# A hand-ordered attention and GELU feed-forward kernel: the order of its arithmetic from the tenth ff tile of batch 0 on is written anew

## The chip, the cores and the metric

One core of a Trainium2 chip. The time is device microseconds (us) of one execution of the whole program. PE is TensorE, DVE is VectorE, ACT is ScalarE, POOL is GpSimd, and SP is the engine that issues the transposing copies, the copies inside the chip and the stores; POOL issues the loads.

## The reference

Sparse attention for 4 batches of 8 heads, 768 positions and 64 columns a head, followed by a feed-forward layer on the 3072 rows of 512 columns:

```python
k_sum = k.reshape(B, H, nb, block, D).max(axis=3)      # blocks of 32 keys
v_sum = v.reshape(B, H, nb, block, D).mean(axis=3)
scores_l = scale * q @ k^T, kept where |i - j| < 16    # a narrow band
scores_s = scale * q @ k_sum^T + log(block)            # 24 block sums
a = softmax over both together
attn = a @ concat(v, v_sum)
...
x = attn.transpose(0, 2, 1, 3).reshape(B * S, H * D)   # 3072 x 512
h = x @ w_in                                           # 512 -> 2048
g = h * sigmoid(1.702 * h)
out = g @ w_out                                        # 2048 -> 512
```

## The kernel before

The kernel runs batch after batch, with the attention of one batch laid between the second product of the batch ahead of it. What is done, and in which order, stands in one long string, `ORDER` (line 35). It is a list of some thousand words. A program walks down it and issues for each word one small step. Every engine gets its steps in the order of the list and works strictly down its own share; engines wait for one another only through the data, through PSUM banks and through buffers that must come free. So moving a word changes the order only on the engines that this word uses, and a step that waits holds all that stands behind it on its engine.

A word is a name and its arguments, with dots between them. The names that matter here:

- `lk`, `lq`, `lv` (POOL): load the keys and queries of one head, or a part of the values, of one batch. `gate.b` (POOL) is a tiny copy that waits until a late transfer has landed, so that the loads behind it do not start earlier.
- `xk.s.g.e`, `xq.s.g` (SP): transposing copies that turn the keys and queries of batches 2 and 3 into the layout that the scores need. `d.half.g` (SP) does so for the attention's output. In batches 0 and 1 this is done on PE instead (`tk`, `tq`, `t`), with a copy out of PSUM (`kc`, `qc`, `c`).
- `xm`, `xa` (DVE): maxima of blocks of keys; `kr`, `kR` write them into the key layout, `kh`, `ka` copy the halo keys there. The last letter of these words is the engine (`d` DVE, `a` ACT, `g` POOL).
- `vm.b.bank` (PE): the block sums of the values, into a PSUM bank; `vb` (DVE): adds them up and writes them to SBUF; `sd`, `ha` (SP): copies of these sums and of the halo values into the value layout `vw`.
- `s.b.half.p.bank` (PE): scores of a pair of heads; `e` (ACT): exponential; `m` (DVE): mask; `v.b.half.p.bank` (PE): the product with the values; `nn.half.g` (DVE): division by the sums, for two pairs.
- `f.half.nt.k...bank` (PE): an ff tile, the first product of the feed-forward layer for 128 of the 2048 columns and half of a batch's positions (four matmuls of 384 columns; `k01` and `k23` are halves of it). `g.half.nt` (ACT): its GELU into `gT`.
- The second product uses Strassen's scheme with seven products in place of eight. `gs.j.n.what` (DVE, or POOL with a `g` at its end) makes the sums of `gT` that it needs, for `n` tiles from `j` on; `ws` the sums of the weights; `p.t.what` (PE) is one of the seven products (eight matmuls of 256 columns) and `x.t.what` takes it out of PSUM, together with what it has to be added to, into one of three output buffers `osb`; `o.b.t.half` (SP) stores such a buffer.
- `G` and `X` (ACT) load the tables for GELU and for the exponential ahead of use.

PSUM is used as four single banks, 0 to 3, and two pairs of banks, 4 and 5. A bank number of two digits means a pair: 42 and 52 are the whole pair 4 or 5, 40, 41, 50 and 51 one bank of it. A step that opens a bank waits until all that used it before has been read out.

A word's batch isn't always in it: the second product of batch 0 is issued among the attention of batch 1, and so on, so that `o.0.2.0` stores the last rows of the first half of batch 0 when the keys of batch 2 are about to be transposed.

Steps that appear later in this text, in the code: `vsum` (line 360) and `block_sums` (372) for `vm` and `vb`, `halos_all` (419) and `rows_all` (427) for `ka` and `kR`, `xk` (649), `xq` (655), `scores` (661), `values` (673), `normed2` (697), `ff` (721), `gelu` (737), `g_sums` (740), `product` (829), `taken` (852), `store` (869). The two lines that open a bank, and the two that rotate the output buffers:

```python
wide_now[where] = psum[where].tile([128, 1024 if dtype is F32 else 2048], dtype, name=name, tag="ps")
...
outp = ctx.enter_context(tc.tile_pool(name="outp", bufs=3))
now[t, o] = outp.tile([128, d_model], F32, name="osb", tag="osb")
```

The loop that walks the list:

```python
for word in ORDER.split():
    name, *args = word.split(".")
    ops[name](*[engines[a] if a in engines else a[1:] if a[0] == "k" else int(a) for a in args])
```

Of the kernel before, what the change touches and what calls it, by code (L numbers as in the profile page):

```python
# [49 lines left out]
f.1.0.k01.2 f.1.8.k23 ha.1.3.0 f.1.9.k0123.0 f.1.0.k23 ws.1.1 g.1.8 g.1.9 f.1.1.k0123.1 ws.2.0 f.1.2.k0123.3 g.1.0  # L50
f.1.3.k0123.2 g.1.1 ws.1.0 gs.0.2.0 ha.1.2.0 f.1.10.k0123.1 g.1.3 gs.0.2.1 f.1.4.k0123.2 g.1.2 gs.2.2.2 g.1.10 lv.1.5.0
gs.0.2.3 f.1.11.k0123.1 g.1.4 f.1.12.k0123.3 g.1.11 f.1.13.k0123.0 ws.3.1 tk.0.52 g.1.13 gs.2.2.0 g.1.12 kc.0.a
f.1.6.k0123.2 gs.0.2.2 gs.2.2.1 f.1.15.k0123.0 f.1.5.k0123.1 ws.3.0 g.1.6 g.1.5 tk.1.52 kc.1.a tk.2.42 kh.0.1.d ws.2.1
f.1.14.k0123.3 f.1.7.k0123.1 tk.3.52 gs.2.2.3 kc.2.a xm.0.1 tq.0.42 gs.4.2.0 g.1.15 kc.3.d p.0.2.0 g.1.7 g.1.14 gs.6.1.0
p.0.1.2 qc.0.a xm.1.1 tq.1.52 ha.1.1.0 gs.4.2.2 lq.2.0 x.0.1.a gs.4.2.1 gs.6.1.2 lq.2.2 gs.6.1.1 gs.7.1.0 ha.1.0.0
qc.1.a gs.6.1.3 lv.2.0.0 tq.2.42 p.1.1.3 qc.2.a gs.7.1.1 gs.4.2.3 p.0.5.1 x.0.5.a p.0.6 tq.3.52 kr.0.1.d s.1.0.0.42
x.0.6.a x.0.2.a gs.7.1.2 X gs.7.1.3 kr.1.1.d x.1.1.d xm.3.1 kh.2.1.g p.1.2.0 e.0.0 p.0.3 p.0.7 lq.2.3 m.0.0 x.0.3.a
x.0.7.a kh.1.1.d qc.3.d s.1.1.0.42 e.1.0 p.1.6 xm.2.1 vm.1.42 o.0.0.0.0.2 s.1.0.1.52 lv.2.5.0 e.0.1 kr.2.1.g kh.3.1.d
p.0.4 vb sd.1.1.0 x.0.4.a gate.1 s.1.1.1.52 e.1.1 lv.2.3.0 p.1.5.1 kr.3.1.d x.1.5.d x.1.2.a m.1.0 x.1.6.a s.1.0.2.52
# [20 lines left out]
lq.3.7 m.1.0 p.1.4 p.2.1.2 v.2.1.0.40 v.2.1.2.50 d.0.0 v.2.1.1.41 v.2.1.3.51 x.2.5.a x.2.1.d x.1.3.a lq.3.3 p.2.6  # L80
o.1.1.0.0.2 x.1.4.d d.0.1 p.2.3 nn.1.0 x.2.6.a p.2.7 nn.1.1 p.2.2.3 x.2.7.a x.2.2.a lv.3.4.0 d.1.0 lv.3.2.1 p.2.4
f.0.9.k01.3 x.2.3.a f.0.1.k01.0 G d.1.1 o.1.2.0.0.2 f.0.1.k23 f.0.8.k01.1 f.0.8.k23 f.0.9.k23 x.2.4.a f.0.0.k01.2
f.0.0.k23 lk.3.6 g.0.1 g.0.9 g.0.8 f.1.1.k0123.0 f.1.8.k0123.1 g.0.0 f.1.9.k0123.3 g.1.1 g.1.9 g.1.8 f.1.0.k0123.2
f.0.10.k0123.0 g.0.10 gate.2 g.1.0 gs.0.2.2 xk.1.1.0 f.1.2.k0123.1 gs.0.2.0.d gs.0.2.1 xk.1.0.1 f.1.10.k0123.3 g.1.2
# [20 lines left out]
g.1.15 gs.7.1.0 gs.7.1.1.g p.0.5.1 x.0.1.d p.0.2.0 p.0.6 x.0.6.a x.0.2.a gs.6.1.3 gs.4.2.2.d x.0.5.d gs.7.1.2 p.1.1.3
p.0.7 p.2.2.0 x.0.7.a x.1.1.a gs.0.2.3.d gs.7.1.3.g gs.4.2.3 p.0.4 x.0.4.a p.0.3 x.0.3.a p.1.2.2 x.1.2.a p.1.6
o.3.0.0.0.2 x.1.6.a p.1.5.1 x.1.5.d o.3.0.1.0.2 p.2.1.2 x.2.1.d p.1.3 x.2.2.a p.1.7 x.1.3.a p.2.6 x.2.6.d x.1.7.a
o.3.1.0.0.2 p.2.5.1 p.2.7 x.2.5.a p.2.3 x.2.7.a p.1.4 p.2.4 x.2.3.a x.1.4.d x.2.4.d o.3.2.1.1.2 o.3.2.0.0.2 P7.0
o.3.1.1.0.2 o.3.2.1.0.1
# [854 lines left out]
```

## Time and profile before

| | |
|---|---|
| median of 3 runs | 212.04 us (211.33 to 214.41) |
| the profiled execution | 211.7 us |
| its span, first to last instruction | 210.0 us |
| mean granted TensorE clock | 0.996 |
| PE busy | 200.4 us |
| DVE busy | 130.8 us |
| ACT busy | 114.3 us |
| POOL busy | 109.1 us |
| ff tiles (`ph`), 512 matmuls | 86.1 us |

All instructions of a compute engine go through one helper, so that the profile gives line 28 for nearly all of them; they are told apart by the tiles that they write and read. `ph` is an ff tile's PSUM bank, `poA`, `poB` and `poC` are those of the second product, `ps_s` of the scores, `ps_av` of the product with the values, `ps_vs` of `vm`. A row of the order of time reads: start, length, engine, operation, what is written and read, how many in a row, and in brackets how long the engine had been idle and what ended that.

### The profile page before, as it was taken

How to read it: one execution, taken by the hardware profiler on the slowest of the kernel's cores; microseconds unless marked ns; L12 is line 12 of the kernel's file. 1: busy time of each engine (PE TensorE's matmuls, PEld its weight loads, DVE VectorE, ACT ScalarE, POOL GpSimd, SP SyncE). 2: the span in 40 equal slices, each digit the busy share in tenths (PEclk: the TensorE clock that was granted, in tenths of full speed). 3: DMA queues.
4: the chain of work that ended last, by engine and by line, in shares of the span. 5: the costliest groups of instructions: out<-in, count | busy, mean ns of one | idle time of the engine just before them, and what ended most of it. 6: DMA issues, size and time to landing. Idle time of an engine off the chain costs nothing.

```text
span 210.0 us, 5880 instructions
## 1 busy us (share of the span) xinstructions
PE 200.4 (95%) x2440; PEld 145.8 (69%) x2440; DVE 130.8 (62%) x311; ACT 114.3 (54%) x227; POOL 109.1 (52%) x157
## 2 busy tenths in 40 slices
PE   7998798999999999999999999999999999999993
PEld 5656554667887886556788865657888865668882
DVE  5577873798997871168997822694888500166342
ACT  2473885659666736676764336567670157671100
POOL 7999972399982998448949422431000000863000
PEclk9999999999999999999999999999999999999998
DMA  4999999999999999999999999939215920000214
GB/s 67 162 166 189 209 213 221 182 144 122 99 134 199 156 177 183 130 126 141 148 166 204 142 227 180 187 29 169 50 53 139 160 105 0 0 3 0 100 53 150
DMA packets 96458, 27.74 MB, mean 132 GB/s; under 512 B 85024, under 2 KB 93488, under 8 KB 96432
## 3 DMA queue, kind: packets, MB, share of 16 engines
q0 software_dynamic: 70800, 13.64, 82.7%
q1 hardware_dynamic: 25632, 13.74, 33.2%
q8 instruction: 19, 0.31, 0.6%
q14 instruction: 7, 0.06, 0.1%
HBM read 27.26 MB, written 6.29 MB: 160 GB/s over the span
## 4 chain that ended last, share of the span: by engine, by line
PE 79%; POOL 12%; DMA 5%; issue 1%; DVE 1%; SPq 0%; POOLq 0%; DVEq 0%
PE ph L28 36%; PE poA L28 19%; PE poB L28 10%; PE poC L28 5%; PE ps_s L28 3%; PE ps_av L28 3%; DMA vw<-vw 2%; POOL mk L28 2%; DMA out_dram<-osb 2%; POOL v0n L28 2%; POOL w_in_sb L28 2%; POOL kb L28 2%; POOL kx L28 2%; POOL qb L28 1%; PE ps_t L28 1%
## 5 line engine op out<-in xcount | busy, mean ns | idle before, releaser
L28 PE MATMUL ph<-xT,w_in_sb 128*128 128x384 f16 x512 | 86.1, 326 | 0.4 <-DVE osb L28 0.4
L28 ACT ACTIVATE gT<-ph 128x384 f16<-128x384 f32 x128 | 56.1, 495 | 30.6 <-PE ph L28 29.9
L28 PEld LDWEIGHTS <-w_in_sb 128*128 128x128 f16 x512 | 49.2, 98 | 32.4 <-issue 0.9
L28 PEld LDWEIGHTS <-gs 128*128 128x128 f16 x384 | 36.5, 98 | 4.6
L28 DVE TENSOR_TENSOR gs<-gT 128x768 f16<-128x768 f16 (+1 forms) x36 | 17.5, 498 | 29.1 <-ACT gT L28 29.0
L28 POOL TENSOR_TENSOR gs<-gs,gT 128x768 f16<-128x768 f16 (+1 forms) x6 | 8.8, 1461 | 41.8 <-PE ph L28 32.7
L28 POOL DMA_DIRECT2D kb<-in_k_dram x28 | 23.1, 842 | 13.7 <-DMA w_out_sb<-in_moe_w_out_dram 6.4
L28 ACT ACTIVATE a_sb<-ps_s 128x768 bf16<-128x768 f32 x32 | 24.8, 808 | 9.5 <-PE ps_s L28 9.3
L28 PEld LDWEIGHTS <-gT 128*128 128x128 f16 x288 | 27.3, 98 | 3.6
L28 POOL DMA_DIRECT2D vw<-in_v_dram x36 | 25.7, 752 | 5.0 <-DMA w_out_sb<-in_moe_w_out_dram 1.7
L28 PE MATMUL poA<-ws,gs 128*128 128x256 f16 x192 | 24.8, 273 | 0.0
L28 POOL DMA_DIRECT2D qb<-in_q_dram x28 | 23.8, 867 | 1.8 <-issue 0.9
L28 DVE TENSOR_TENSOR a_sb<-a_sb,mk 128x768 bf16<-128x768 bf16 x28 | 14.7, 550 | 3.0 <-ACT a_sb L28 2.2
L28 DVE TENSOR_TENSOR x<-ps_av,rc 128x768 f16<-128x768 f32 (+1 forms) x18 | 15.6, 869 | 0.6
L28 ACT ACTIVATE s<-poA 128x256 f32<-128x256 f32 x14 | 5.4, 382 | 19.3 <-PE poA L28 18.6
L28 PE MATMUL poB<-ws,gs 128*128 128x256 f16 x96 | 12.5, 273 | 0.0
L28 PE MATMUL poC<-w_out_sb,gT 128*128 128x256 f16 x96 | 12.5, 273 | 0.0
L28 PE MATMUL poA<-w_out_sb,gT 128*128 128x256 f16 x96 | 12.4, 273 | 0.0
L28 PE MATMUL poB<-w_out_sb,gs 128*128 128x256 f16 x96 | 12.4, 273 | 0.0
L28 PE MATMUL poA<-ws,gT 128*128 128x256 f16 x96 | 12.3, 273 | 0.0
L28 DVE TENSOR_REDUCE ka<-kx 128x48 bf16<-128x1536 bf16 x4 | 7.0, 1750 | 7.4 <-DMA kx<-kb 7.4
L28 ACT ACT_TABLE_LOAD x8 | 10.3, 1283 | 0.9 <-PEq L948 0.8
(102 smaller groups left out, 219.0 us busy)
## 6 DMA issues: line engine op xcount, KB each, us to landing
out_dram<-osb SPq DMA_DIRECT2D x23, 256.0 KB, 2.9
kb<-in_k_dram POOLq DMA_DIRECT2D x24, 96.0 KB, 6.0
qb<-in_q_dram POOLq DMA_DIRECT2D x24, 96.0 KB, 5.0
vw<-in_v_dram POOLq DMA_DIRECT2D x36, 64.0 KB, 5.1
w_out_sb<-in_moe_w_out_dram POOLq DMA_DIRECT2D x4, 512.0 KB, 14.8
w_in_sb<-in_moe_w_in_dram POOLq DMA_DIRECT2D x3, 512.0 KB, 11.3
vw<-vs SPq DMA_DIRECT2D x6, 198.0 KB, 3.9
kb<-in_k_dram POOLq DMA_DIRECT2D x4, 192.0 KB, 4.4
```

The costliest lines, as they stand in the source:

```text
L28: r = f(*a, **kw)
```

## The change

Only the string `ORDER` changes. It holds the same 1002 words before and after, none added, none taken away, none with another argument: every step keeps its engine, its bank and its size. Up to the word `lq.1.4` (the 180th) nothing moves at all, and on PE the first ten ff tiles and `f.0.11` keep their places. Behind that the order of the steps on PE, ACT and DVE is new. The order of all copies that SP issues and of all loads that POOL issues is the same as before. On POOL some steps of arithmetic (`kh.2.1`, `kr.2.1`, `ka.0`, and a few of the `gs`) stand elsewhere between the loads.

Much of it are exchanges of neighbours. The wider moves, as the words run on one engine:

```diff
 # PE, batch 0, first values
-f.0.8 f.0.9 f.0.11 f.0.10 v.0.1.0 v.0.1.1 v.0.1.2 f.0.13 f.0.12 t.1.0 v.0.1.3 f.0.15 f.0.14 t.1.1
+f.0.8 f.0.9 f.0.11 v.0.1.0 v.0.1.2 v.0.1.3 v.0.1.1 f.0.15 f.0.10 f.0.13 f.0.12 t.1.0 t.1.1 f.0.14
 # PE, end of batch 0's second product
-v.1.0.2 v.1.0.3 v.1.1.2 v.1.1.3 p.2.4 f.0.1.k01 t.0.1 f.0.9.k01 f.0.8.k01 f.0.0.k01
+p.2.4 v.1.0.2 v.1.0.3 p.2.2 t.1.0 f.0.0.k01 t.0.1 f.0.9.k01 f.0.1.k01 v.1.1.2 v.1.1.3 f.0.1.k23 p.2.3
 # DVE, the same place
-nn.0.0 nn.1.0 x.2.7 x.2.2 m.1.2 x.2.3 nn.0.1 nn.1.1 c.0.1 c.1.1
+nn.0.0 m.1.3 x.2.7 nn.1.0 nn.0.1 x.2.2 c.0.1 nn.1.1 x.2.3 c.1.1
 # DVE, ahead of batch 2's scores
-xa.0.0 gs.2.2.0 vb gs.2.2.1 gs.2.2.3 xa.1.0 gs.7.1.0 kR.0
+xa.0.0 vb gs.2.2.0 gs.2.2.1 gs.2.2.3 gs.4.2.2 gs.0.2.3 gs.4.2.0 gs.7.1.0 xa.1.0 kR.0
 # PE, batch 1's second product
-p.1.2 p.1.7 p.1.3 p.1.4 p.2.1 v.2.1.0 v.2.1.2 v.2.1.1 v.2.1.3 p.2.6
+p.1.2 p.1.3 p.1.6 v.2.1.2 v.2.1.0 v.2.1.1 v.2.1.3 p.2.1 p.1.7 p.2.6
 # PE, batch 2's ff tiles
-f.1.3 vm.3 f.0.13 f.0.3 ... f.1.15 f.0.7 s.3.0.1 s.3.0.0 p.0.2 p.0.1 p.1.2 p.0.5
+f.1.3 f.0.11 f.0.4 ... f.0.14 f.1.6 vm.3 f.1.15 f.0.15 f.1.7 p.0.1 p.1.2 s.3.0.1 s.3.0.0 p.0.5
 # DVE, the same place
-gs.0.2.3 xa.0.1 vb xa.1.1 kR.1 gs.2.2.0 ka.1 gs.2.2.3 gs.6.1.0 gs.6.1.1 gs.4.2.0
+gs.0.2.3 gs.6.1.0 ka.1 gs.6.1.2 kR.1 gs.6.1.1 gs.4.2.0 vb x.0.1 gs.7.1.0
 # POOL
-lq.2.0 lq.2.2 lv.2.0.0 kh.2.1 lq.2.3 lv.2.5.0 kr.2.1 gate.1
+lq.2.0 lq.2.2 kh.2.1 lv.2.0.0 kr.2.1 lq.2.3 lv.2.5.0 gate.1
 # PE, last batch
-f.1.7 f.1.15 f.0.15 p.0.1 p.0.5 p.0.2 p.0.6
+f.1.7 f.1.15 f.0.14 p.0.5 p.0.1 p.1.1 p.0.6 f.0.15 p.0.7 p.0.2
```

`P7.0`, which only gives memory back, stands somewhat earlier in the list, and `late`, which opens two pools, ahead of `m.1.3` as before.

More of the change, by code (lines that the diff above doesn't have):

```diff
@@ L50 @@
[L50 to L59, printed above, removed]
@@ L80 @@
[L80 to L84, printed above, removed]
@@ L105 @@
[L105 to L109, printed above, removed]
+lk.1.5 lk.1.6 lq.1.2 lk.1.7 m.1.1 lq.1.1 lv.1.0.0 lq.1.4 cv.1 lq.1.5 lq.1.7 lv.1.3.1 f.0.8.k0123.2 lq.1.6 lv.1.0.1
@@ new lines @@
+lv.1.2.0 lv.1.1.0 lv.1.1.1 lv.1.4.0 lv.1.2.1 lv.1.4.1 late g.0.8 f.0.9.k0123.3 f.0.11.k0123.0 g.0.11 m.1.3 v.0.1.0.40
+v.0.1.2.50 v.0.1.3.51 v.0.1.1.41 f.0.15.k0123.0 ws.0.0 g.0.9 f.0.10.k0123.1 nn.1.0 f.0.13.k0123.3 nn.1.1 g.0.10
+f.0.12.k0123.2 g.0.13 t.1.0.42 t.1.1.52 f.0.14.k0123.1 ha.1.3.0 g.0.12 c.1.0.d g.0.14 f.1.0.k01.2 f.1.8.k01.3 c.1.1.d
+f.1.8.k23 ws.1.0 g.1.8 ha.1.2.0 f.1.1.k0123.1 g.0.15 ws.0.1 g.1.1 f.1.0.k23 f.1.2.k0123.3 f.1.10.k0123.1 g.1.0 lv.1.3.0
+ws.3.0 g.1.2 f.1.3.k0123.2 g.1.10 f.1.9.k0123.0 ws.1.1 g.1.3 ws.3.1 f.1.11.k0123.1 f.1.4.k0123.2 g.1.9 f.1.13.k0123.0
@@ new lines @@
+x.0.6.a gs.4.2.3 x.0.5.a lq.2.0 qc.1.a xm.1.1 p.0.3 s.1.0.0.42 xm.3.1 tq.3.52 kr.1.1.d e.0.0 kh.3.1.d p.0.7 vm.1.42
+qc.3.d s.1.0.1.52 x.0.3.a ha.1.0.0 lq.2.2 o.0.0.0.0.2 x.0.7.a p.1.2.0 vb kh.2.1.g kr.3.1.d x.1.2.a p.0.4 p.1.5.1 x.1.6.a
+e.0.1 lv.2.0.0 m.0.0 s.1.1.1.52 x.0.4.a e.1.1 xm.2.1 m.1.0 x.1.5.d kr.2.1.g sd.1.1.0 s.1.0.3.42 e.0.3 p.1.7 s.1.0.2.52
+p.2.1.2 lq.2.3 e.0.2 lv.2.5.0 p.1.3 x.1.7.a x.2.1.a gate.1 lv.2.3.0 s.1.1.3.42 lv.2.1.1 m.0.1 s.1.1.2.52 m.0.3 lk.2.0
+e.1.2 lk.2.2 m.0.2 lv.2.2.0 e.1.3 p.2.6 sd.1.0.0 p.1.4 x.1.3.a v.1.0.0.50 m.1.2 o.0.0.1.0.2 lv.2.2.1 x.2.6.a lk.2.3
@@ new lines @@
+x.2.2.a f.0.0.k01.2 lv.3.2.1 x.2.3.a f.0.9.k01.3 f.0.8.k01.1 d.1.1 f.0.8.k23 g.0.8 f.0.9.k23 f.0.1.k23 g.0.9 o.1.2.0.0.2
+lk.3.6 f.0.0.k23 g.0.0 f.1.8.k0123.1 xk.1.1.0 xk.1.0.1 g.0.1 g.1.8 f.1.9.k0123.3 f.1.0.k0123.2 gate.2 g.1.9 g.1.0
+f.1.1.k0123.0 o.1.1.1.0.2 g.1.1 gs.0.2.0.d f.1.10.k0123.3 f.0.2.k0123.2 g.1.10 g.0.2 f.0.10.k0123.0 f.1.2.k0123.1
+xk.1.1.1 g.0.10 f.1.11.k0123.3 f.0.13.k0123.0 f.0.3.k0123.2 g.1.2 f.1.3.k0123.1 g.0.13 g.0.3 xk.1.0.0 g.1.3
+f.0.11.k0123.0 xa.0.1 g.1.11 f.0.4.k0123.2 gs.0.2.1 lq.3.6 gs.0.2.2 f.1.12.k0123.3 g.0.11 f.0.12.k0123.1 xa.1.1 lv.3.5.1
@@ L110 @@
+p.2.1.2 x.1.5.d p.1.3 x.2.1.d o.3.0.0.0.2 o.3.0.1.0.2 p.2.2.0 p.1.7 p.2.6 x.1.3.a x.1.7.a x.2.6.d o.3.1.0.0.2 p.2.5.1
+x.2.5.a p.2.7 p.2.3 x.2.2.a x.2.7.a o.3.2.1.1.2 p.1.4 x.2.3.a o.3.2.0.0.2 x.1.4.d p.2.4 o.3.1.1.0.2 x.2.4.d o.3.2.1.0.1
 """
```

89 lines of the change are left out of this document (45 added, 44 removed).

## The prediction

> **What bounds the kernel now.** I read the page first, then busy time by stretch, then the chain that ended last, then the order of time on PE and DVE.
>
> ```profile
> PE 200.4 (95%) x2440; PEld 145.8 (69%) x2440; DVE 130.8 (62%) x311; ACT 114.3 (54%) x227; POOL 109.1 (52%) x157
> ```
>
> In the second view the first number after the stretch is its length and the next is PE's busy time in it.
>
> ```profile
> 33.40:34.80 1.40, 0.35 (x9) 0.25 (x10) 0.22 (x1) 0.73 (x2) 0.60 (x1) 1.00 1.24 217
> 34.80:100.30 65.50, 65.50 (x803) 46.48 (x800) 46.72 (x99) 41.91 (x83) 48.62 (x66) 1.00 1.78 150
> 100.30:122.50 22.20, 21.77 (x353) 18.66 (x353) 18.34 (x43) 10.72 (x18) 13.85 (x19) 1.00 1.92 177
> 122.50:123.20 0.70, 0.29 (x3) 0.11 (x2) 0.57 (x2) 0.38 (x1) 0.00 (x0) 1.00 1.28 284
> 123.20:206.40 83.20, 83.20 (x832) 60.92 (x831) 42.34 (x91) 40.26 (x85) 17.76 (x15) 1.00 0.44 87
> 206.40:210.00 3.60, 0.00 (x1) 0.00 (x0) 0.42 (x1) 0.00 (x0) 0.00 (x0) 0.79 0.38 139
> ```
>
> From 33.4 us on, where the changed part begins, PE is idle 1.05 + 0.43 + 0.41 = 1.89 us before its last matmul, at a granted clock of 1.00, and then 3.6 us pass for the last eviction and store. The change keeps every matmul. So at most 1.9 us can be won, under 1%, while any new wait of PE is paid in full. The question is which of the three gaps close and where new ones open.
>
> **The prices.** The chain of waits gives PE's, in the order start, length, what; behind it two rows of PE's timeline.
>
> ```profile
> 39.33 7.51 PE ph L28 x44
> ...
> 75.52 0.88 PE ps_av L28 x48
> ...
> 131.71 0.53 PE ps_vs L28 x48
> ...
> 167.26 20.80 PE ph L28 x128
> 188.06 0.87 PE poA L28 x8
> ```
>
> ```profile
> 33.73 0.19 PE L28 MATMUL ps_av<-vw,a_sb 128*64 128x65 bf16 x1 [0.28 <-DVE ws L28]
> 34.69 0.73 PE L28 MATMUL ps_av<-vw,a_sb 128*64 128x65 bf16 x35 [0.77 <-DMA vw<-vw]
> ```
>
> An ff tile (4 matmuls) is 20.80/128 x 4 = 0.65 us, a `p` 0.87, a `v` 0.88/4 = 0.22, the value sums `vm` 0.53. With these I add up the PE list of both orders.
>
> **First place, `v.0.1.x`.** The second matmul of `v.0.1.0` waits for a halo copy that releases it at 34.69. Nothing ahead of that copy changes. Before, four ff tiles (8, 9, 11, 10) run first and PE waits 0.28 + 0.77; after, tile 10 stands behind the `v`, so PE arrives 0.65 earlier and waits 0.65 more. Some returns: from 34.69 to 39.33 PE runs 47 `v` matmuls, four ff tiles and two `t` in seven pieces in 4.64 us, against 0.86 + 2.60 + 0.67 = 4.13 at the dense price (a `t` at 0.33, an estimate: six matmuls of 128 columns by the 20.80/128 of 384 columns). Half as many changes of kind should give back some 0.2 of these 0.5. Term: +0.45 (0.3 to 0.65).
>
> **Second place, the transposes for batch 2.** In the SP list nothing moves, but what it waits for does. `xk.0.0.0`, the first of six transposing copies, stands behind `o.0.2.0` and `o.0.2.1`. DVE's rows, then SP's:
>
> ```profile
> 75.56 0.43 DVE L28 TENSOR_TENSOR osb<-poB,s 128x256 f32<-128x256 f32 x1 [0.32 <-PE poB L28]
> ...
> 77.24 0.22 DVE L28 RECIPROCAL rc<-ps_av 128x12 f32<-128x12 f32 x1
> 77.50 0.96 DVE L28 TENSOR_TENSOR x<-ps_av,rc 128x768 f16<-128x768 f32 x1
> ```
>
> ```profile
> 77.82 0.33 SPq L28 DMA_DIRECT2D out_dram<-osb  x1
> 78.41 8.40 SPq L28 DMA_TRANSPOSE kx<-kb  x4
> 86.90 10.33 SPq L28 DMA_TRANSPOSE qT<-qb  x2
> ```
>
> Before, `x.2.3` is done at 75.99, `x.2.4` lets `o.0.2.1` go at 77.82, and `xk` starts at 78.41. After, `x.2.3` stands on DVE behind `nn.1.1`, which needs `v.1.1.3`, which ended at 76.40. Ahead of that `v` PE now also runs `p.2.4`, three half ff tiles and `t.0.1`, and no longer `p.2.3`: +0.87 + 0.98 + 0.33 - 0.87 = 1.31. With the 0.45 it ends at 78.2; `nn.1.1` takes 77.50 + 0.96 - 77.24 = 1.22, `x.2.3` 0.43, so `o.0.2.0` goes at 79.85, `o.0.2.1` 0.59 later, `xk` another 0.59 later: 81.0, 2.6 later than before. Queued behind it on SP are all six transposes and the six `ha`/`sd` copies of batch 2. The last two transposes, alone in their windows, and the last `ha`:
>
> ```profile
> L28 SPq DMA_TRANSPOSE qT<-qb x1: 5776/5776/5776, 86.9 to 86.9; - x1
> ...
> DMA to landing us min/median/max: 12.1/12.1/12.1
> ```
>
> ```profile
> L28 SPq DMA_TRANSPOSE qT<-qb x1: 1518/1518/1518, 95.7 to 95.7; - x1
> ...
> DMA to landing us min/median/max: 7.6/7.6/7.6
> ```
>
> ```profile
> L28 SPq DMA_DIRECT2D vw<-vw x1: 1337/1337/1337, 102.2 to 102.2; - x1
> ...
> DMA to landing us min/median/max: 8.6/8.6/8.6
> ```
>
> `xq.0.1` lands at 103.3. Its first reader before was `s.2.0.2`:
>
> ```profile
> 100.79 0.66 PE L28 MATMUL ps_s<-qT,kx 64*128 64x64 bf16 x24 [0.43 <-issue]
> ...
> 104.11 0.52 PE L28 MATMUL ps_s<-qT,kx 64*128 64x64 bf16 x24
> ```
>
> It has 0.8 us to spare. After, `s.2.0.3` takes this place at the same depth of the PE list, due at 104.35 (0.45 from above, 0.2 less from the next term). How much of the 2.6 reaches the landing no row shows. At 0 it lands at 103.3 and costs nothing; in full at 105.9 and costs 1.55, and the last `ha`, landing at 102.2 + 8.6 = 110.8 before, comes as late for `v.2.0.2`, due near 112.0 then. SP was free for `xq.0.1` at 86.90 + 5.78 = 92.7 and issued it at 95.7, so a shift of 2.6 still fits ahead of that issue, which speaks for less than the full shift. I take half: 104.6, so 0.25, and 0.35 for the `ha`. Term: +0.6 (0 to 2.7).
>
> On this the Trainium skill, "DMA: Bandwidth & Descriptors", section "Queues, rings and completion order", says that each DMA engine takes turns, packet by packet, between the queues that have work. By that rule loads drain faster while SP is silent and the late transposes share with fewer of them; the term would be nearer 0.3 than 0.6. No row of this execution separates the two.
>
> **Third place, `s.2.0.x`.** The 0.43 at 100.79 is `kR.0` on DVE, late behind `xa.1.0`. After, `p.0.1` stands ahead of the scores too. From the end of `vm.2` to the first score PE has eight ff tiles and two `p`, 6.95 us; DVE has `vb`, six sums of 768 columns, one of 384, `xa.1.0` and `kR.0`, by the rows of the fourth place 1.52 + 2.8 + 0.27 + 1.75 + 0.45 = 6.8. A near tie, at worst 0.4 more when the late transposes hold `xa.0.0` ahead of `vb`. Term: -0.2 (-0.43 to +0.3).
>
> **The gap at 122.5.**
>
> ```profile
> 122.63 0.42 DVE L28 TENSOR_TENSOR osb<-poC,s 128x256 f32<-128x256 f32 x1 [1.16 <-DMA out_dram<-osb]
> ```
>
> `x.2.2` waits for a free output buffer, that is for `o.1.1.0`, issued after `x.1.3`. `p.1.3` moves 1.75 up the PE list (two `p`), so the buffer comes free about as much earlier, and the wait was 1.16. Term: -0.4 (-0.4 to 0).
>
> **Fourth place, `vm.3` and `vb` of batch 3.** Before, `vm.3` runs at 131.6 and `vb` right after it. After, `vm.3` is ten us further down the PE list, behind `f.1.6`, and on DVE `vb` stands behind `gs.6.1.0` (which needs `f.1.6`), `ka.1`, `gs.6.1.2`, `kR.1`, `gs.6.1.1` and `gs.4.2.0`. `vm.3` fills PSUM bank pair 5, which `s.3.0.0.52` takes next, so that score must wait for the end of `vb`. DVE's rows; a later row's start shows how fast each is followed:
>
> ```profile
> 135.44 0.28 DVE L28 COPY vpart<-ps_vs 128x128 f32<-128x128 f32 x1
> ...
> 136.96 1.75 DVE L28 TENSOR_REDUCE ka<-kx 128x48 bf16<-128x1536 bf16 x1
> 138.75 0.53 DVE L28 COPY kx<-ka 128x576 bf16<-128x576 bf16 x2
> 139.20 0.55 DVE L28 TENSOR_TENSOR gs<-gT 128x768 f16<-128x768 f16 x1
> 139.66 2.10 DVE L28 COPY kx<-kx 128x320 bf16<-128x320 bf16 x3
> 141.69 0.55 DVE L28 TENSOR_TENSOR gs<-gT,gs 128x768 f16<-128x768 f16 x1
> ...
> 143.78 0.35 DVE L28 TENSOR_TENSOR gs<-gT,gs 128x384 f16<-128x384 f16 x1
> 144.05 0.35 DVE L28 TENSOR_TENSOR gs<-gT 128x384 f16<-128x384 f16 x1
> 144.61 0.36 DVE L28 TENSOR_TENSOR gs<-gT 128x384 f16<-128x384 f16 x1 [0.21 <-ACT gT L28]
> ```
>
> ```profile
> 144.09 1.26 ACT L28 ACTIVATE gT<-ph 128x384 f16<-128x384 f32 x3 [0.69 <-PE ph L28]
> ```
>
> One gelu is 0.495 and is handed on in 0.03 (144.09 to 144.61). So from the end of `f.1.6`: gelu with both handovers 0.57; sum of 384 columns 0.27; `ka.1` 141.69 - 139.66 = 2.03; sum 0.27; `kR.1` 0.45; sum 0.27; sum of 768 columns 0.46; `vb` 136.96 - 135.44 = 1.52; handover 0.05: 5.89 us. PE meanwhile: `vm.3` 0.53, three ff tiles 1.95, `p.0.1` and `p.1.2` 1.74, one `s`, half of the 0.52 at 104.11, 0.26: 4.48. PE waits 1.4 us. Queued behind it: `p.0.5` and all that follows. Nothing hides it, since PE has no spare time later. Upper end with each sum at its full length and `ka` at 2.10: 2.0; lower end with 0.1 for each of three changes of kind on PE: 1.1. The scores' `sd` copies come ten us later as well but stay ahead of `v.3.0.2`, eight `p` further on. Term: +1.4 (1.1 to 2.0).
>
> **What costs nothing.** On POOL the loads keep their order; `kr.2.1` now stands ahead of two of them (some 1.5 us), and behind them `gate.1` holds the queue anyway:
>
> ```profile
> 67.04 0.18 POOL L28 COPY gate<-vw 32x1 bf16<-32x1 bf16 x1 [4.16 <-DMA vw<-vs]
> ```
>
> In the last batch `p.0.5` follows `f.0.14` directly; its eighth matmul comes 0.65 + 0.76 = 1.41 after `f.1.15`, the gelu and two sums that it needs take 0.57 + 0.27 + 0.36 + 0.05 = 1.25. No wait, 0.16 to spare; 0.4 if that cover is gone.
>
> **Sum.** 0.45 + 0.6 - 0.2 - 0.4 + 1.4 = +1.85 us. The profiled execution took 211.7 us, a span of 210.0 and 1.7 around it: 213.55. The median of the runs shown, 212.04, is 0.34 above that execution, so I predict 213.9.
>
> **Rivals.** *Late transposes decide.* If `xq.0.1` meets the traffic that `xq.0.0` met and takes 12.1 us instead of 7.6, it lands at 95.7 + 12.1 = 107.8, and `s.2.0.3` waits 3.45 instead of the 0.6: +4.7, 216.7. For it: both lengths are in the trace, and the loads of batch 3 begin just there. Against it: before, the same copy had 7.6 at the same issue time. It makes the whole slower by over 2% (4.24 us) when the landing passes 107.35, or 106.75 with the fourth place at its upper end. *The waits fall away.* If `vb` costs PE nothing, because bank pair 5 or the DVE list is free earlier than I add up, and the transposes land as before: 0.45 - 0.2 - 0.4, 211.9. For it: only 1.4 us of cover is missing. Against it: DVE runs strictly down its list, and `ka.1` cannot pass `gs.6.1.0`. *Faster by over 2%* would need 4.24 us where PE has 1.89 of idle time to give; only a shift of the measurement could show it. That the change does not do what it says, and every wait stays as it was, gives 212.0 and is counted with the second rival.
>
> **Chances.** Forecast (213 to 216) 0.44, late transposes 0.36, waits fall away 0.18, faster by over 2% 0.02. Two per cent is about what a measurement of this kernel can tell from no change. So: faster 0.02, within 2% 0.62, slower 0.36. The range runs from the second rival, 212.0, to the first with a little of the full shift on top, 217.6.
>
> **What would show it.** Right: PE idle before the `v` at 33 us near 1.7; `xk` starting near 81; no gap before the ff tiles near 123; PE waiting some 1.4 us for DVE `vs` between the two scores at 146 to 148. Wrong: no gap there, or PE idle over 2 us at `s.2.0.3` near 105, which is the first rival; or a gap in a place not named here, which means a dependence that I did not see.

## The result and the profile after

The changed kernel takes 213.51 us (median of 22 runs, 211.82 to 215.57), the kernel before 212.18 (22 runs, 210.23 to 214.74) on the same chip. Both have some executions in a slower state (3 of these 22 for the changed kernel); without them the ratio is 1.0085, 95% interval 1.0061 to 1.0108, which is 1.8 us, while the two medians differ by 1.3. So the change makes the kernel slower, by less than 2%. The profiled execution took 213.88 with a span of 212.2, 2.2 more than the span before. The forecast was +1.85 and 213.9. So the total was met, but only two of its six terms were: some were too large by about as much as others were too small, and that is luck.

Section 1 of the page after, TensorE's and the other engines' busy time:

```profile
PE 200.3 (94%) x2440; PEld 145.2 (68%) x2440; DVE 133.8 (63%) x311; ACT 116.5 (55%) x227; POOL 110.7 (52%) x157
```

PE does the same work (200.4 before). DVE has the same 311 instructions and needs 3.0 us more for them (130.8 before), POOL 1.6 more for its 157. An unchanged count with more busy time means that single operations became longer. Busy time by stretch of the changed kernel (after the stretch its length, then PE's busy time):

```profile
32.50:36.00 3.50, 2.32 (x56) 1.74 (x57) 1.80 (x3) 0.68 (x2) 0.82 (x1) 1.00 1.24 210
36.00:100.30 64.30, 64.20 (x760) 45.94 (x758) 45.26 (x100) 42.97 (x84) 48.37 (x66) 1.00 1.74 150
100.30:123.50 23.20, 21.30 (x348) 17.87 (x347) 19.15 (x42) 10.98 (x19) 14.05 (x19) 1.00 1.94 169
...
145.00:160.00 15.00, 14.89 (x250) 12.33 (x249) 14.21 (x37) 10.42 (x16) 1.16 (x1) 1.00 0.28 68
160.00:208.60 48.60, 47.56 (x409) 35.67 (x407) 23.49 (x41) 17.81 (x41) 10.85 (x7) 1.00 0.24 64
```

The waits behind these losses, in PE's timeline of the changed kernel (in brackets the idle time ahead of a row and what ended it):

```profile
32.94 0.19 PE L28 MATMUL ps_av<-vw,a_sb 128*64 128x65 bf16 x1 [0.67 <-DMA vw<-vw]
33.87 0.92 PE L28 MATMUL ps_av<-vw,a_sb 128*64 128x65 bf16 x47 [0.73 <-DMA vw<-vw]
...
102.62 0.67 PE L28 MATMUL ps_s<-qT,kx 64*128 64x64 bf16 x24 [1.90 <-issue]
...
192.49 0.61 PE L28 MATMUL poA<-ws,gs 128*128 128x256 f16 x4 [0.90 <-DVE gs L28]
```

Against the execution before: first place 1.40 instead of 1.05; batch 2's first score 1.90 instead of 0.43; the gap of 0.41 near 123 gone; between 145 and 160 us, where 1.4 was forecast, 0.11; and 0.90 at `p.0.6` of the last batch, a place that the prediction doesn't name. +0.35 + 1.47 - 0.41 + 0.11 + 0.90 = +2.4, against 2.2 in the span.

What DVE does ahead of the first score of batch 2 (its timeline, the changed kernel):

```profile
95.39 0.56 DVE L28 TENSOR_TENSOR gs<-gT 128x768 f16<-128x768 f16 x1
95.98 0.69 DVE L28 TENSOR_TENSOR gs<-gs,gT 128x768 f16<-128x768 f16 x1
96.71 0.69 DVE L28 TENSOR_TENSOR gs<-gT,gs 128x768 f16<-128x768 f16 x1
97.32 1.57 DVE L28 TENSOR_TENSOR gs<-gT 128x768 f16<-128x768 f16 x1
...
100.01 1.74 DVE L28 TENSOR_REDUCE ka<-kx 128x48 bf16<-128x1536 bf16 x1
101.79 0.94 DVE L28 COPY kx<-ka 128x576 bf16<-128x576 bf16 x2
```

and POOL beside it (the first row issues a load, the second is `ka.0`):

```profile
95.55 0.82 POOL L28 DMA_DIRECT2D kb<-in_k_dram  x1 [2.69 <-DMA kx<-kb]
96.37 2.10 POOL L28 COPY kx<-kx 128x320 bf16<-128x320 bf16 x3
```

From the end of the value sums at 95.39 to `xa.1.0` at 100.01 six sums of 768 columns and one of 384 take 4.62 us, priced at 2.8 + 0.27; `kR.0` takes 0.86 up to its successor at 102.65, priced at 0.45. The sum at 97.32, three times as long as its neighbours of the same shape, ends 0.4 behind POOL's copies. Theory 1: a DVE operation that reads two SBUF tiles, or copies within SBUF, waits for a POOL instruction that it meets. Its rivals: the list is merely longer than was added up, or late transposes hold the scores.

### The profile page after: what moved, and what is told of

The parts are those of the page before. It is cut to its first block, busy times and chain, and to the rows that moved or that the text cites. A ratio compares the mean times of both kernels' runs of the same rounds, so it can differ in the third digit from the quotient of the medians.

```text
span 212.2 us, 5878 instructions
## 1 busy us (share of the span) xinstructions
PE 200.3 (94%) x2440; PEld 145.2 (68%) x2440; DVE 133.8 (63%) x311; ACT 116.5 (55%) x227; POOL 110.7 (52%) x157
## 5 line engine op out<-in xcount | busy, mean ns | idle before, releaser
L28 ACT ACTIVATE gT<-ph 128x384 f16<-128x384 f32 x128 | 57.8, 493 | 29.9 <-PE ph L28 29.2
L28 DVE TENSOR_TENSOR gs<-gT 128x768 f16<-128x768 f16 (+1 forms) x36 | 19.4, 560 | 28.8 <-ACT gT L28 28.6
L28 POOL DMA_DIRECT2D qb<-in_q_dram x28 | 23.3, 844 | 2.4 <-DMA kb<-in_k_dram 1.1
L28 DVE TENSOR_TENSOR gs<-gT,gs 128x768 f16<-128x768 f16 (+1 forms) x19 | 12.4, 672 | 1.9 <-POOL gs L28 1.8
```

Source lines behind the costliest of these rows:

```text
L28: r = f(*a, **kw)
```

## The experiments

All but two (one that leaves out a sum of POOL, and a small kernel that only times single operations) keep all work. Where a ratio is given it is to the kernel before on the same chip.

**The tail: one sum taken off POOL.**

```diff
-gs.4.2.1 x.0.5.d p.0.6 x.0.6.a f.0.15.k0123.0 g.0.15 gs.2.2.2.g p.0.7
+gs.4.2.1 gs.2.2.2.d x.0.5.d p.0.6 x.0.6.a f.0.15.k0123.0 g.0.15 p.0.7
```

> The changed kernel with the last batch's gs.2.2.2 on DVE right behind gs.4.2.1 instead of on POOL behind gs.7.1.1. All work kept; nothing ahead of gs.4.2.1 on DVE or ahead of p.0.6 on TensorE is touched. Theory 1 (POOL's sum stretches DVE's): gs.4.2.1 falls from 1.66 to 0.5 to 0.6, the wait of 0.90 at p.0.6 (192.49) to 0 to 0.1, no new wait at p.0.7, the time falls 0.6 to 0.9 us. Rival (gs.4.2.1 is long because its input, POOL's gs.4.2.0 or the last gelus, comes late): 1.66 and the 0.90 stay, the time moves less than 0.2.

212.27 us, ratio 1.0012 (0.9967 to 1.0056), against 1.0085 for the changed kernel, and the two intervals don't meet. DVE's `gs.4.2.1` in the changed kernel, POOL's `gs.2.2.2` beside it, then DVE's row here:

```profile
190.77 1.66 DVE L28 TENSOR_TENSOR gs<-gs,gT 128x768 f16<-128x768 f16 x1
```

```profile
190.26 1.75 POOL L28 TENSOR_TENSOR gs<-gT 128x768 f16<-128x768 f16 x1
```

```profile
190.54 0.54 DVE L28 TENSOR_TENSOR gs<-gs,gT 128x768 f16<-128x768 f16 x1
```

1.66 becomes 0.54 and the wait of 0.90 at `p.0.6` is gone. It stands in all eight profiles that leave this stretch as the change has it, with 0.89 or 0.90. Nothing ahead of this sum moved, so its order isn't what made it long: the rival falls here.

**Batch 2's halo copies of the keys taken off POOL.**

```diff
-g.0.7 ka.0.g lv.3.1.1
+g.0.7 ka.0.d lv.3.1.1
```

> The changed kernel with the three halo copies ka.0 of batch 2 on DVE instead of POOL, at their place in the order (behind gs.7.1.0, ahead of xa.1.0). All work kept. Theory 1 (DVE's sums of two SBUF tiles are stretched by POOL's copies beside them): POOL is clear, gs.4.2.2 falls from 1.57 to about 0.55, the two sums of 0.69 to 0.55, ka.0 costs DVE 0.65 as ka.1 does in the changed kernel, kR.0 ends 0.4 to 0.9 us earlier, and the wait of 1.90 at the first score of batch 2 falls to 1.0 to 1.5 although DVE has more to do. Rival (the list is merely longer than the prediction added up, each piece at its own price): gs.4.2.2 stays near 1.5, DVE has 0.65 more, the wait grows to about 2.5 and the time by 0.6.

212.85 us, ratio 1.0052 (1.0021 to 1.0082); this interval meets the changed kernel's, so a gain in time isn't shown. DVE's timeline:

```profile
97.16 0.55 DVE L28 TENSOR_TENSOR gs<-gT 128x768 f16<-128x768 f16 x1
...
98.84 0.65 DVE L28 COPY kx<-kx 128x320 bf16<-128x320 bf16 x3
```

`gs.4.2.2` (the row at 97.16) takes 0.55, all seven sums 3.34 us (95.50 to 98.84), and the score waits 0.59 although DVE has more to do. The same is seen without an edit at this place: in the run with POOL's sum doubled, told below, this stretch is the changed kernel's, but POOL got to `ka.0` earlier.

```profile
94.73 1.61 POOL L28 COPY kx<-kx 128x320 bf16<-128x320 bf16 x3
```

There it was over at 96.34, when DVE's first sum had just begun (96.14): the sums took 0.55 to 0.62 and the score waited 0.25. In the seven profiles with this stretch unchanged the wait is 0.25 to 1.90, mean 1.13, and it goes with where `ka.0` falls: begun a microsecond or more ahead of DVE's first sum it left 0.25 and 0.64, begun between 0.22 ahead and 0.98 behind it 1.13 to 1.90. The 1.90 of the profile after is the far end; in two profiles of the order before it was 0.43 and 0.93.

**The order of `kR.0` alone undone.**

```diff
-lk.3.0 gs.2.2.3 g.1.7 ... xq.0.1 xa.1.0 kR.0.d p.0.2.0
+lk.3.0 gs.2.2.3 xa.1.0 kR.0.d g.1.7 ... xq.0.1 p.0.2.0
```

> The changed kernel with one edit: xa.1.0 and kR.0 of batch 2 go back on DVE from behind gs.7.1.0 to right behind gs.2.2.3, where they stood between four sums before. All work kept. In the changed kernel TensorE waits 1.90 us at the first score of batch 2 (102.62), released with nothing named, while DVE works through six sums, xa.1.0 and kR.0. Theory 1 (that wait is the DVE list, whichever the reason for its length): kR.0 ends near 100 instead of 102.7, the wait falls from 1.90 to 0 to 0.5, perhaps 0.3 us returns at p.2.5, the time falls 1.2 to 1.9 us to about 212. Rival (late transposes: what the score waits for is the landing of xk or xq): the wait stays at 1.6 to 1.9, the time moves less than 0.3.

213.89 us in the median of four, ratio 1.012 (1.0057 to 1.0183): nothing won, where 1.2 to 1.9 us were expected. PE's timeline (this execution took 215.51, the longest of the four):

```profile
103.74 0.39 PE L28 MATMUL poB<-ws,gs 128*128 128x256 f16 x2 [0.36 <-DVE gs L28]
104.74 1.27 PE L28 MATMUL poB<-ws,gs 128*128 128x256 f16 x10 [0.61 <-DVE gs L28]
```

The wait at the score is 0, and 0.36 + 0.61 open at `p.2.5` and 0.29 more at `p.0.6`, which read the sums that now stand behind `kR.0`. So the scores wait for DVE's list and not for the landing of a transpose (the late transposes fall as their direct cause), and the order of the list only chooses who waits.

**POOL's sum done twice, then three times, under `ka.1`.** The first was to bring the forecast's missing wait at 146 to 148 us back.

```diff
-x.0.1.d gs.2.2.2.g g.1.15
+x.0.1.d gs.2.2.2.g gs.2.2.2.g g.1.15
```

> The changed kernel with one instruction more: POOL does gs.2.2.2 of batch 3 twice in a row, so that it is busy for some 1.7 us more from 143.6, when DVE runs ka.1 (143.72). The second sum writes the same values. Theory 1 (the 2.03 us at which the prediction priced ka.1 was a duration beside a busy POOL, and the predicted wait of 1.4 at s.3.0.0 is missing because POOL is idle there now): ka.1 takes 1.8 to 2.1 us instead of 0.65, vb ends 1.1 to 1.5 later, a wait of 0.9 to 1.5 opens between the first two scores of batch 3, the time rises 0.9 to 1.4 us. Rival (ka.1 is short for another reason, such as its operands or its neighbours on DVE): ka.1 stays at 0.65, no wait opens, the time moves less than 0.3.

213.75 us, ratio 1.0103 (1.0057 to 1.0149). Missed: `ka.1` stayed at 0.65. The sum of 384 columns ahead of it took 1.48 us instead, ending 0.2 behind POOL's, and PE waited 0.92 at the score. DVE's rows, then POOL's:

```profile
142.37 1.48 DVE L28 TENSOR_TENSOR gs<-gT 128x384 f16<-128x384 f16 x1 [3.53 <-ACT gT L28]
143.77 0.65 DVE L28 COPY kx<-kx 128x320 bf16<-128x320 bf16 x3
```

```profile
140.30 3.34 POOL L28 TENSOR_TENSOR gs<-gT 128x768 f16<-128x768 f16 x2
```

So `ka.1` doesn't take 2 us of its own at that place; the operation of DVE that meets POOL pays. With a third sum:

> The changed kernel with POOL doing gs.2.2.2 of batch 3 three times in a row (the second and third sum write the same values), so that POOL sums from about 138.5 to 145.3. With two of them the wait went to gs.6.1.0 (128x384, 1.48 us, ending 0.2 us behind POOL's second sum) and ka.1 stayed at 0.65. Theory 1, sharpened (a DVE operation of two SBUF inputs, or a SBUF copy, that meets a running sum of POOL ends only when that sum ends): gs.6.1.0 ends behind the second sum, ka.1 then meets the third and takes 1.2 to 2.1 us instead of 0.65, vb ends 1.1 to 1.6 later against TensorE, the wait between the first two scores of batch 3 grows to 1.6 to 2.6 us, the time rises 0.9 to 1.6 us over the changed kernel's. Rival (stretched by a constant share while both run, or not by POOL at all): ka.1 and the sums behind it stay under 1.0 us each, the wait stays at 0.3 to 0.9, the time within 0.4.

217.31 us, ratio 1.0241 (1.0145 to 1.0337). DVE's, POOL's and PE's timelines:

```profile
142.47 3.54 DVE L28 COPY kx<-kx 128x320 bf16<-128x320 bf16 x3
145.94 0.34 DVE L28 TENSOR_TENSOR gs<-gT 128x384 f16<-128x384 f16 x1
```

```profile
140.57 5.23 POOL L28 TENSOR_TENSOR gs<-gT 128x768 f16<-128x768 f16 x3
```

```profile
146.56 0.54 PE L28 MATMUL ps_s<-qT,kx 64*128 64x64 bf16 x12 [0.59 <-DVE kx L28]
148.93 0.50 PE L28 MATMUL ps_s<-qT,kx 64*128 64x64 bf16 x12 [1.83 <-DVE vs L28]
149.36 1.89 PE L28 MATMUL poB<-ws,gs 128*128 128x256 f16 x8
```

The same three copies take 3.54 us instead of 0.65 and end 0.2 behind POOL's third sum at 145.80; the next sum is back at 0.34. The predicted wait is there at last, 0.59 + 1.83. The time rose more than expected, for a reason told in the last section.

**The row that the prediction priced `ka.1` by.** The kernel before, its `gs.2.2.1` of batch 3 left out:

```diff
-f.0.14.k0123.0 gs.2.2.1.g f.0.6.k0123.2
+f.0.14.k0123.0 f.0.6.k0123.2
```

> The kernel before without POOL's gs.2.2.1 of batch 3 (left out: that quarter of one group of sums keeps the values of the batch before). In the kernel before this sum runs 139.84 to 141.55 on POOL and ka.1 139.66 to 141.76 on DVE, 2.10 us, the row from which the prediction took 2.03. Theory 1: ka.1 takes 0.6 to 0.7 here. Rival (2.1 is what the three copies cost at that place): 1.9 to 2.1. TensorE has no wait there in either case; the time stays within 0.5.

211.71 us in one run (the kernel before 212.65). POOL's sum in the kernel before, then DVE's timeline in this run:

```profile
139.84 1.71 POOL L28 TENSOR_TENSOR gs<-gs,gT 128x768 f16<-128x768 f16 x1 [3.12 <-DVE gs L28]
```

```profile
139.81 0.66 DVE L28 COPY kx<-kx 128x320 bf16<-128x320 bf16 x3
```

2.10 becomes 0.66 with nothing else changed around it. The length of the row that the prediction quoted was that of POOL's sum, not that of the copies.

**The dispute measured by itself.**

> A kernel of its own that computes nothing of the reference (it writes zeros to the output): for each of six kinds of DVE operation, six in a row, alone (none), beside five sums of two fp16 SBUF tiles of 128x768 on POOL (sum), beside five fp16 copies of 128x768 on POOL (copy), and beside four loads issued by POOL (dma). The kinds: a sum of two fp16 SBUF tiles of 128x768 (tt) and of 128x384 (half), a fp16 SBUF copy of 128x768 (cp), a max reduction of 128x1536 bf16 (red), a copy of 128x256 fp32 from PSUM (ps), a sum of PSUM and SBUF 128x256 fp32 (pa). Theory 1 (DVE and POOL take turns at something that a DVE operation with two SBUF inputs, or a fast SBUF copy, needs whole): tt, half and cp take about 0.5, 0.3 and 0.3 us alone and about as long as POOL's operation beside sum, 1.2 to 2 us; ps, pa and red stay within 10% of their lengths alone; dma changes none of them by more than 0.4 us an operation. Rival (a general contention for SBUF's bandwidth): all kinds that read or write SBUF, red and pa among them, lengthen by a like share, and tt by less than 2 times.

Groups by operation and shape (out<-in, shapes, count, busy time, mean ns of one; the end of the name tells what ran on POOL):

```profile
L28 POOL TENSOR_TENSOR wsum<-c,d 128x768 f16<-128x768 f16 x30 | 49.9, 1664 | 2.4
L28 POOL COPY wcopy<-c 128x768 f16<-128x768 f16 x30 | 25.9, 863 | 1.8
...
L28 DVE TENSOR_REDUCE ored_sum<-r 128x48 bf16<-128x1536 bf16 x6 | 10.5, 1752 | 0.2
...
L28 DVE TENSOR_TENSOR ott_sum<-a,b 128x768 f16<-128x768 f16 x6 | 9.9, 1651 | 0.2
L28 DVE COPY ocp_sum<-a 128x768 f16<-128x768 f16 x6 | 8.7, 1458 | 0.2
L28 DVE TENSOR_TENSOR ohalf_sum<-a,b 128x384 f16<-128x384 f16 x6 | 8.7, 1457 | 0.2
...
L28 DVE TENSOR_TENSOR ott_dma<-a,b 128x768 f16<-128x768 f16 x6 | 3.3, 558 | 0.2
L28 DVE TENSOR_TENSOR ott_none<-a,b 128x768 f16<-128x768 f16 x6 | 3.3, 557 | 0.2
...
L28 DVE COPY ocp_none<-a 128x768 f16<-128x768 f16 x6 | 2.2, 359 | 0.2
```

Mean ns of one DVE operation:

| kind | alone | beside sums | beside copies | beside loads |
|---|---|---|---|---|
| sum of two SBUF tiles, 768 | 557 | 1651 | 976 | 558 |
| the same, 384 | 356 | 1457 | 776 | 358 |
| copy in SBUF, 768 | 359 | 1458 | 777 | 420 |
| max reduction | 1751 | 1752 | 1752 | 1752 |
| copy from PSUM | 423 | 423 | 423 | 423 |
| sum of PSUM and SBUF | 422 | 423 | 423 | 422 |

A long and a short sum both come to about the length of POOL's operation (1664 and 863): the two engines take turns, one DVE operation per POOL operation, and it is POOL's length that is paid. What reads PSUM, and the reduction, isn't touched. That rules out the rival, a share of SBUF's bandwidth common to all.

**Batch 3's sums taken off POOL.**

```diff
-f.0.15.k0123.0 gs.2.2.1.g kR.1.d ... x.0.1.d gs.2.2.2.g g.1.15
+f.1.14.k0123.3 gs.0.2.3 gs.2.2.1 gs.2.2.2 g.0.12 ... f.0.15.k0123.0 kR.1.d ... x.0.1.d g.1.15
```

> The changed kernel with batch 3's gs.2.2.1 and gs.2.2.2 on DVE right behind gs.0.2.3, where DVE has 2.65 us free before gs.6.1.0, instead of on POOL. All work kept. Theory 1 (what is left of the predicted wait at s.3.0.0 is gs.6.1.0 standing behind POOL's second sum): gs.6.1.0 takes 0.35, ka.1 0.65, and the wait between the first two scores of batch 3, which was 0 to 0.92 in four executions with this stretch unchanged, is 0 to 0.1; the time falls 0.2 to 0.6 us. Rival (the missing 0.05 us of cover, or the order with its two changes of kind on TensorE, keeps a wait): 0.3 or more stays.

`gs.6.1.0` takes 0.36, `ka.1` 0.66, and PE is busy for all of 145 to 160 us. But the time is 213.97 us, ratio 1.0081 (1.0042 to 1.0121), no better than the changed kernel's: the mechanism shows, its worth in time doesn't. With the stretch unchanged the wait was 0, 0, 0, 0.11, 0.27 and 0.67, so little was to be won.

**The first place undone.**

```diff
-g.0.11 m.1.3 v.0.1.0.40 ... g.0.9 f.0.10.k0123.1 nn.1.0
+g.0.11 m.1.3 f.0.10.k0123.1 v.0.1.0.40 ... g.0.9 nn.1.0
```

> The changed kernel with one ff tile, f.0.10, back ahead of v.0.1.0 on TensorE (its gelu stays where it is). All work kept. Theory (the halo copy sets when v.0.1.0 can go on, and the changed order has one tile of 0.65 less ahead of it): the idle time at the two v rows falls from 1.40 to about 0.75, the time by 0.3 to 0.6 us, part of it lost again by one more change of kind. Rival (the landing moves with the transfers and not with the order, so that TensorE meets it as late whatever runs ahead): the idle time stays at 1.2 to 1.6 and the time within 0.2.

213.30 us, ratio 1.0038 (1.0006 to 1.007) against the changed kernel's 1.0085; the intervals meet. PE's timeline:

```profile
33.52 0.19 PE L28 MATMUL ps_av<-vw,a_sb 128*64 128x65 bf16 x1 [0.15 <-DMA vw<-vw]
34.46 0.92 PE L28 MATMUL ps_av<-vw,a_sb 128*64 128x65 bf16 x47 [0.74 <-DMA vw<-vw]
```

0.89 of idle time instead of 1.40. Over all profiles the mean is 1.40 with three tiles ahead of `v.0.1.0` (eight profiles, 1.04 to 1.97) and 0.57 with four (five profiles, 0 to 1.05). The landing varies by about 1 us, the difference is near one tile.

**The second place: the start of the transposes moved.**

```diff
-o.0.2.0.0.2 c.1.1.d g.0.9 o.0.2.1.0.2 ... xk.0.0.0 ... xk.0.0.1
+xk.0.0.0 xk.0.0.1 o.0.2.0.0.2 c.1.1.d g.0.9 o.0.2.1.0.2 ...
```

> The changed kernel with xk.0.0.0 and xk.0.0.1, the first two transposing copies of keys for batch 2, ahead of the stores o.0.2.0 and o.0.2.1 on SyncE's queue. All work kept. In the prediction a start of xk 2.6 us later was worth 0 to 2.7 us, for which 0.6 was taken; in the changed kernel xk started 1.6 later than before and xq.0.1 landed at 101.9 against 103.3 before. Theory (xq.0.1 is issued when the load lq.2.7 has landed, at 95.0 to 95.7 in both, and not when SyncE is free; so the start of xk sets nothing): xk starts 2 us or more earlier, xq.0.1 is still issued within 0.7 of 95.2, no wait opens or closes at batch 2's scores beyond the 0.25 to 1.90 that executions differ by there, the time stays within 0.4. Rival (the transposes pass a shift on in full): xq.0.1 is issued and lands 1.5 to 2.5 us earlier, and the wait at the first score falls with it.

213.29 us, ratio 1.0081 (1.005 to 1.0112); the wait at the first score is 1.13. `xk` starts at 78.29, 1.7 earlier than in the changed kernel, `xq.0.1` is issued at 94.3, 0.9 earlier and so a little outside what was expected, and lands at 102.6, 0.7 later. What its issue follows is a load. In the changed kernel, `lq.2.7` on POOL and `xq.0.1` on SyncE (duration, start; then the time to landing):

```profile
L28 POOL DMA_DIRECT2D qb<-in_q_dram x1: 909/909/909, 85.4 to 85.4; - x1
...
DMA to landing us min/median/max: 9.6/9.6/9.6
```

```profile
L28 SPq DMA_TRANSPOSE qT<-qb x1: 1444/1444/1444, 95.2 to 95.2; - x1
...
DMA to landing us min/median/max: 6.7/6.7/6.7
```

The load lands at 85.4 + 9.6 = 95.0 and the transpose is issued at 95.2. Before it is 84.6 + 11.0 = 95.6 and 95.7, here 84.2 + 10.0 = 94.2 and 94.3. `xk` started at 78.4, 80.0 and 78.3 in these three. So the start of `xk` sets neither this issue nor a wait of the queries' readers. It does reach another place: the load right ahead of `ka.0` on POOL waits until the last transposing copy of the keys has landed (the row at 95.55 above). That was at 95.0 in the changed kernel and at 93.7 here, and `ka.0` began at 96.37 and 95.07. A transfer thus helps to decide which of DVE's sums `ka.0` meets, and the wait at the first score with it; how much that is worth was not tried.

**Everything together.** The tail, the first place and batch 3's sums as above, `ka.0` on DVE, and:

```diff
-gs.4.2.2.d ... gs.0.2.3 ... gs.6.1.0 X x.0.1.d
+gs.6.1.0 gs.4.2.2.d gs.0.2.3 X x.0.1.d
```

> The changed kernel with what the runs point to, all work kept: f.0.10 ahead of v.0.1.0; batch 2's ka.0 on DVE, and its gs.4.2.2 and gs.0.2.3 behind gs.6.1.0, since their readers come later; batch 3's gs.2.2.1 and gs.2.2.2 on DVE behind gs.0.2.3; the last batch's gs.2.2.2 on DVE behind gs.4.2.1. Theory 1: idle time at the first v rows 0.75 instead of 1.40, at batch 2's first score 0 to 0.3 instead of 1.90, between batch 3's first scores 0 to 0.1, at p.0.6 of the last batch 0; the time falls 2.5 to 3.5 us to 210.0 to 211.0, 0.5 to 1.0% under the kernel before. Rival (TensorE meets the next late operation as soon as one wait is gone, as it did when xa.1.0 and kR.0 were moved alone): new waits of 1 us or more, no faster than the kernel before.

212.06 us (12 runs), ratio 1.0010 (0.9979 to 1.0041): what the change lost is back, 0.7% or some 1.6 us under it (1.0010/1.0085) where 2.5 to 3.5 were expected, and the kernel before isn't beaten. PE's waits from 32.5 us on:

```profile
35.02 0.92 PE L28 MATMUL ps_av<-vw,a_sb 128*64 128x65 bf16 x47 [0.53 <-DMA vw<-vw]
...
101.70 0.71 PE L28 MATMUL ps_s<-qT,kx 64*128 64x64 bf16 x24 [0.29 <-DVE kx L28]
...
106.16 0.39 PE L28 MATMUL poA<-ws,gs 128*128 128x256 f16 x2 [0.68 <-DVE gs L28]
```

The tail and batch 3 wait no more; in batch 2 DVE still sets the pace. These waits come to 1.50 us, against 1.89 in the profile before, and yet the span is 0.7 longer (210.7): in the first 33 us, which the orders have in common but for a few steps, PE is busy 27.48 us here and 28.91 there. What differs so early from execution to execution was not looked into. A last version puts the sums that are read late behind those read early:

```diff
-gs.2.2.3 ... gs.6.1.0 gs.4.2.2.d gs.0.2.3 ... gs.7.1.3 gs.4.2.3 ... gs.6.1.1 gs.7.1.2 ... gs.6.1.3 gs.6.1.2.d m.0.2 gs.0.2.2.d
+gs.6.1.0 ... gs.6.1.1 gs.7.1.2 gs.0.2.3 gs.2.2.3 gs.4.2.3 gs.6.1.3 gs.7.1.3 ... gs.6.1.2.d gs.4.2.2.d m.0.2 gs.0.2.2.d
```

> The changed kernel with the edits of the run named best and a further one in the stretch of batch 2's scores, where DVE then still set the pace (waits of 0.29 at the first score and 0.68 at the last two matmuls of p.0.6): the sums that only p.0.3 and p.0.7 read (gs.0.2.3, gs.2.2.3, gs.4.2.3, gs.6.1.3, gs.7.1.3, gs.4.2.2) stand on DVE behind gs.6.1.1 and gs.7.1.2, which p.0.6 reads. All work kept. Theory (there DVE does first what is read last): both waits fall to 0 to 0.1, no new one of more than 0.3 at p.0.3, the time falls 0.6 to 1.0 us below that of best, to about 211.2, 0.2 to 0.6% under the kernel before. Rival (DVE is saturated between 94 and 108 us, so the wait moves on to p.0.3 or to the first v of batch 2): 0.6 to 1.0 us of new waits, the same time as best.

213.03 us, ratio 1.0067 (1.0035 to 1.0099): worse than the version before it, where the rival had it equal. The wait moved on, as the rival said, to a place that neither named:

```profile
109.09 1.83 PE L28 MATMUL poA<-ws,gs 128*128 128x256 f16 x8 [1.87 <-DVE gs L28]
```

PE comes to `p.0.7` earlier and finds `gs.0.2.2` still behind a mask: two short waits became one of 0.17 and one of 1.87, and the matmuls behind it are slow. This execution took 214.25, 1.2 above the median of its kind, so what a usual one loses isn't shown.

## Why the prediction was right in its sum and wrong in its terms

By its own signs the prediction was wrong in its parts: there is next to no gap between the two scores at 146 to 148, and there is one in a place that it doesn't name.

- **First place, +0.45:** +0.35 in the two profiles; 0.83 between the means of many, above the range of 0.3 to 0.65. Right in mechanism; the 0.2 that fewer changes of kind should give back can't be seen.
- **Second place, +0.6:** 0. `xq.0.1` landed at 101.9, 1.4 earlier than before, and no wait stands at `s.2.0.3`, nor at `v.2.0.2` for the last `ha`. `xk` did start later, by 1.6 and not 2.6. The failed step is "I take half": `xq.0.1` is released by the load `lq.2.7`, and SyncE being free at 92.7 and issuing at 95.7 was the sign of it. The load's landing and this issue go together in two further runs too (96.6 and 96.8 with `kR.0` undone, 95.0 and 95.1 with everything together). The rival "late transposes decide" falls with it. The Trainium skill, "DMA: Bandwidth & Descriptors", "Queues, rings and completion order", pointed to the lower value; the landings lie on that side, but the load's landing is what explains the issue.
- **Third place, -0.2:** +1.47 in the two profiles, some +0.5 between the means (1.13 against 0.43 and 0.93). The failed step is the sum 6.8, made of lengths without POOL beside them. DVE needed 1.53 + 4.62 + 1.78 + 0.86 = 8.8 us there. 8.8 - 6.95 of cover is 1.85, the wait of 1.90. Of the 2.0 too little, 1.3 came with `ka.0` on POOL (without it the seven sums take 3.34), most of it in the one sum of 1.57, and 0.3 is the price of the sums themselves. The 0.4 of `kR.0` is not settled: it took 0.53 to 0.94 in different runs. Loads issued by POOL changed a copy by 0.06 in the small kernel, but with everything together the three copies of `ka.0` took 1.04 on DVE with nothing but loads on POOL.
- **The gap at 122.5, -0.4:** -0.41, gone in every profile with the new order (0.41 and 0.69 in two of the old). Right.
- **Fourth place, +1.4:** +0.11, and 0.18 in the mean of six profiles. The failed step is `ka.1` at 2.03, read from a row beside POOL's sum. With its own length the list is 5.89 - 2.03 + 0.57 = 4.43 against 4.48 of cover, a tie. In the new order POOL's sums come ahead of `ka.1` and end at 143.58; only `gs.6.1.0` meets them (0.67).
- **The tail, 0:** +0.90. `p.0.5` was looked at and has no wait; `p.0.6`, which reads `gs.4.2.1`, was not.

Taken between the means of all profiles with the same order at a place, the terms that came are 0.83 + 0 + 0.45 - 0.55 + 0.18 + 0.90 = +1.8, as much as the ratio says. They fall otherwise than in the two profiles, and the luck of the sum is the same.

Three of the four misses (third place, fourth place, tail) lie in one mechanism: a length was taken from, or carried to, a place without asking what POOL did beside it. That made one term too large and two too small. The Trainium skill, "SBUF — State Buffer", section "SBUF: two separate sides", states the rule that was missed: DVE and GpSimd share one pair of ports by an exclusive lock, which a GpSimd operation holds for a whole instruction, and so does a DVE operation in a mode that uses two ports, or one with two SBUF inputs against a GpSimd operation that reads SBUF. The trace agrees: 557 ns became 1651 beside operations of 1664, and nothing changed for PSUM sources. By that rule the row of 2.10 in the profile before, with POOL's 1.71 beside it, would have been read as the copies' own length and a wait for POOL, and with the 0.65 that the runs show the fourth place comes to about 0.

## What to carry to other kernels

Before a DVE duration is used in a sum, see what POOL runs in the same microseconds, both where the row is from and where it goes: the same three copies took 0.65, 2.10 and 3.54 us here. When an order is changed, every pair of a DVE sum and a POOL sum is a new one, so a list that keeps each engine's work can still lengthen it. A forecast whose total is met should be opened term by term: this one, by the two profiles, was right through 2.0 us that were priced and didn't come (0.1 + 0.6 + 1.3) and 2.6 that came and weren't priced (1.7 + 0.9).
